# A first stage issued in the order of its text, with the weight splits of the second stage set behind it

## The chip, the cores and the metric

The kernel runs on one core of one Trainium2 chip. The metric is the device time of one execution in microseconds (us). The core has a matrix engine (PE), a vector engine (DVE), an activation engine (ACT), GpSimd (POOL) and a sync engine (SP) whose queue issues the DMAs. Each engine takes its instructions from a queue of its own, in the order in which they stand there.

## The reference, cut to what matters

```python
def _attn_ref(r, k, v, w, u):                 # 4 batches, 8 heads, 768 steps, 48 wide
    for t in range(S):
        cur = einsum('bhd,bhe->bhde', u[None] * kt, vt)
        y[:, :, t] = einsum('bhd,bhde->bhe', rt, state + cur)
        state = wt[:, :, :, None] * state + einsum('bhd,bhe->bhde', kt, vt)

x = attention as 3072 tokens x 384
h = maximum(maximum(x @ w1, x @ w2), x @ w3)   # 384 -> 768
x = h @ w_out                                  # 768 -> 384
h = x @ w_in                                   # 384 -> 2048
out = (h - tanh(h)) @ w_out2                   # 2048 -> 384
```

Weights come as float64 and are turned to float32 on the chip.

## The kernel before, in words

The attention is cut into 24 chunks of 128 steps, six for each batch, and the tokens into six groups of four chunks (512 tokens). Chunks 0 to 3 are computed first. Then group 0 goes through the first two layers while chunks 4 to 7 are computed in between, then group 1 with chunks 8 to 11, and so on. After the six groups a last stage runs the layer of 2048.

A chunk is prepared one chunk ahead, on DVE: two scans over the decays (`scans`, into the single buffers `suf` and `fwd`), two multiplications of keys and receptance (`decays`), and a product for the term with `u` (`bonus`). ACT squares the scans for a range test (`squares`), PE sums the bonus (`bonus_sum`), POOL decays the state (`state_decay`). Then, for the chunk itself, PE makes the scores into banks 4 and 5 (`scores`) and transposes the keys into bank 7 (`key_turn_pe`), ACT copies the keys to `kcn` and the scores to `P` (`masked`), POOL zeroes half of each `P`, DVE puts the bonus on its diagonal from chunk 6 on (`diagonal`), PE adds keys and values to the state (`state_mm`) and computes the outputs (`outputs`), and ACT takes them out (`outputs_out`, for which the first chunks need one copy over 96 partitions and three over 32). From chunk 8 on the keys are turned by a DVE transpose and a trip through DRAM (`key_turn`, `key_order`) and not on PE.

Group 0 uses float32 weights `WAg` and `WOg` as they come. One unit is 128 x 384 weights: `w1_load` fetches it, `w1_unit` converts it, one ACT instruction (L66) and four on DVE (L72 to L75). There are 18 units of `WAg` and 6 of `WOg`. In group 0 a unit of `WAg` feeds three matmuls (L639), a slot; the maximum over three slots goes to `h0`, and 18 matmuls over `WOg` (L666) end the group. Later groups use each weight as two parts, high and low: `wA_split` and `wO_split` (both `split`, L433 and L434) make them from `WAg` and `WOg`, a cast on ACT and a subtraction on POOL (even units) or DVE (odd units). Every matmul of the later groups needs its unit's two parts (L443 to L445).

The text gives an order, but what stands in a queue is decided when the program is built: a scheduler sets each instruction where it reckons the engine to be free, so an instruction can stand before others that precede it in the text. The splits of `WAg` and `WOg`, which the text has after the group's last matmuls, stand much earlier in the queues that way.

`PRELOAD` says how many weight units are fetched ahead of chunk 2's loads and how many before chunk 3's, `PRO` how many are converted after each of chunks 0 to 3, `LEAD` how many slots ahead of PE a unit is converted in group 0:

```python
PRO = [0, 1, 3, 4]
LEAD = 3
PRELOAD = [1, 6]
                w1_upto(slot + 1 + LEAD + max(0, slot - 8))
```

Of the kernel before, what the change touches and what calls it, by code (L numbers as in the profile page):

```python
# [10 lines left out]
F32R = mybir.dt.float32r  # L11
# [8 lines left out]
P = 128  # L20
# [19 lines left out]
EARLY_R = [0, 5]  # L40
W2A = 12
MM_BANKS = [0, 1, 2, 3]
PRO = [0, 1, 3, 4]
LEAD = 3
WARM = [12, 4, 2, 0]
PRELOAD = [1, 6]
SLOTS = 8
AC = 64 + HD
VW = NP * 3 * HD
# [42 lines left out]
def main_path(ctx, tc, wT, rkT, w0, rk0, nat, vpad, uT, ub, wA, wo1, wi2, wo2, outT, count):  # L92
# [85 lines left out]
    def ring(c):  # L178
        return c % 3
# [91 lines left out]
    def key_turn_pe(c):  # L271
        if needs_state(c):
            for p in range(NP):
                pe.transpose(dsb[:, p * C:(p + 1) * C], rk[ring(c)][:, 1, p, :], ident)
            act.copy(kcn.rearrange("t b r -> t (b r)"), dsb)


# [97 lines left out]
    def att_steps(c, col):  # L375
        n = c + 1 if c + 1 < NCH else None
        st = {}

        def k0():
            scores(c, st)  # L380
            masked(c, st)
            if n and n < EARLY_B:
                bonus(n)
            if n:
                scans(n)

        def k1():
            if c < KEYS_PE:
                key_turn_pe(c)
            if c >= EARLY_B:  # L390
                diagonal(c)
            if n:
                decays(n)
                if n >= EARLY_B:
                    bonus(n)
                squares(n)

        def k2():
# [12 lines left out]
        def k4():  # L411
            outputs(c)
            outputs_out(c, col)
            if n and n < EARLY_B:
                bonus_vals(n)
            load_next(c)

        return [k0, k1, k2, k3, k4]

    def in_range():  # L420

# [33 lines left out]
    def warm(n):  # L455

        for _ in range(n):
            pe.matmul(bank[3], zeros[:, 0:P], zeros, start=True, stop=True)

    zeros = xs[:, KT - 1, 256:512].bitcast(BF16)  # L460
    pool.memset(zeros, 0.0)
    warm(WARM[0])
# [16 lines left out]
    def w1_load(i):  # L479
        sp.dma_start(Yi[:, (i % SLOTS) * 2 * UN:(i % SLOTS + 1) * 2 * UN], w1raw[i].bitcast(I32))  # L480
# [43 lines left out]
    for c in range(GROUPS[0]):  # L524
        st = {}
        n = c + 1
        scores(c, st)
        key_turn_pe(c)
        masked(c, st)
        warm(WARM[2] if c < 2 else 0)  # L530
        state_mm(c)
        bonus(n)
        scans(n)
        decays(n)
        state_add(c)
        state_decay(n)
        outputs(c)
        warm(WARM[3] if c < 2 else 0)
        outputs_out(c, c * C)
        squares(n)  # L540
        load_next(c)
        if c == 0:
            sp.dma_start(ubt, ub)
            for i in range(PRELOAD[1], SLOTS):
                w1_load(i)
        for _ in range(PRO[min(c, len(PRO) - 1)]):
            w1_unit()
        bonus_sum(n)
        bonus_vals(n)
# [38 lines left out]
    def y_split(g, d):  # L588
# [2 lines left out]
        act.copy(hi[:, d], src)  # L591
        dve.tensor_tensor(lo[:, d], src, hi[:, d], ALU.subtract)

    c0 = 0
    for g, gn in enumerate(GROUPS):
        n = gn * C
        lastg = g == len(GROUPS) - 1
        nchunks = [] if lastg else list(range(c0 + gn, c0 + gn + GROUPS[g + 1]))
        steps = [s for i, c in enumerate(nchunks) for s in att_steps(c, i * C)]
        nslots = 3 * F1  # L600
        if g == len(GROUPS) - 2:
            def w2_open():
# [18 lines left out]
        def advance(slot):  # L621
            nonlocal done
            want = min(len(steps), -(-len(steps) * (slot + 1) // nslots))
            while done < want:
                if steps[done]:
                    steps[done]()
                done += 1
            if g == 0:
                w1_upto(slot + 1 + LEAD + max(0, slot - 8))
            if g == 1:  # L630
                wA_split(slot + 1 + SPLIT_LEAD)

        slot = 0
        for f in range(F1):
            for j in range(3):
                bk = mm()
                for k in range(KT):
                    if g == 0:
                        pe.matmul(bk, WAg[3 * f + j][:, k], x0[:, k], start=k == 0, stop=k == KT - 1)  # L639
                    else:  # L640
                        mm3(bk[:, 0:n], WAh[:, f, j, k], WAl[3 * f + j][:, k], xh[:, k, 0:n], xl[:, k, 0:n],
                            k == 0, k == KT - 1)
                if j == 0:
                    t = tmp()
                    act.copy(t[:, 0:n], bk[:, 0:n])
                else:
                    dve.tensor_tensor(h0[:, f] if g == 0 and j == 2 else t[:, 0:n], bk[:, 0:n], t[:, 0:n], ALU.max)  # L647
                if j == 2 and g:
                    act.copy(hh[:, f, 0:n], t[:, 0:n])  # L649
                    (dve if f == F1 - 1 else pool).tensor_tensor(hl[:, f, 0:n], t[:, 0:n], hh[:, f, 0:n], ALU.subtract)  # L650
                advance(slot)
                slot += 1
        if lastg:
# [7 lines left out]
            w2_queue(units)  # L661
        for d in range(KT):
            bk = mm()
            for f in range(F1):
                if g == 0:
                    pe.matmul(bk, WOg[:, d, f], h0[:, f], start=f == 0, stop=f == F1 - 1)  # L666
                    continue
                mm3(bk[:, 0:n], WOh[:, d, f], WOl[:, d, f], hh[:, f, 0:n], hl[:, f, 0:n], f == 0, f == F1 - 1)
            if lastg:
                y_split(0, d)  # L670
                w2_step()
            elif d == 0:
                if g == 0:
                    xh = shared.tile([P, KT, 512], F32R, name="xh", tag="xh")
                x_split(GROUPS[g + 1] * C)
            act.copy(ys(d, g), bk[:, 0:n])  # L676
            if g == 0:
                wO_split(2 * d)
                wO_split(2 * d + 1)
                wA_split(SPLIT_B * (d + 1))  # L680
        if g == 0:
            hh, hl = (shared.tile([P, F1, 512], F32R, name=t, tag=t) for t in ("hh", "hl"))
# [242 lines left out]
```

## Time and profile before

| what | us |
|---|---|
| median of 3 runs | 881.69 (881.02 to 881.86) |
| the profiled execution | 885.45 |
| its span, first to last instruction | 883.7 |
| PE busy | 847.8 |
| DVE busy | 503.3 |
| ACT busy | 328.6 |
| POOL busy | 196.4 |

Busy time is the union of an engine's instructions. Matmuls are pipelined and their ends are modelled, so that a stretch in which PE waits a little inside a row of matmuls still reads as busy. The granted clock of PE is given as a share of its full 2.4 GHz; its other level is 1.2 GHz.

### The profile page before, as it was taken

How to read it: one execution, taken by the hardware profiler on the slowest of the kernel's cores; microseconds unless marked ns; L12 is line 12 of the kernel's file. 1: busy time of each engine (PE TensorE's matmuls, PEld its weight loads, DVE VectorE, ACT ScalarE, POOL GpSimd, SP SyncE). 2: the span in 40 equal slices, each digit the busy share in tenths (PEclk: the TensorE clock that was granted, in tenths of full speed). 3: DMA queues.
4: the chain of work that ended last, by engine and by line, in shares of the span. 5: the costliest groups of instructions: out<-in, count | busy, mean ns of one | idle time of the engine just before them, and what ended most of it. 6: DMA issues, size and time to landing. Idle time of an engine off the chain costs nothing.

```text
span 883.7 us, 11938 instructions
## 1 busy us (share of the span) xinstructions
PE 847.8 (96%) x4482; PEld 650.9 (74%) x4482; DVE 503.3 (57%) x824; ACT 328.6 (37%) x647; POOL 196.4 (22%) x201
## 2 busy tenths in 40 slices
PE   7889689999999999999998999999999999999996
PEld 5755344777777777778876688888888888888884
DVE  8879893674574764747999734334334334333332
ACT  4554432334334243335455423234223224323222
POOL 6443560352442442420253300000000000000000
PEclk8799889999999999999999999999999999999999
DMA  9555323234235244215534100000000000000001
GB/s 266 149 208 161 106 80 96 75 104 145 69 115 140 76 129 134 83 25 155 145 98 137 36 0 36 1 1 36 1 1 36 0 1 36 1 0 36 1 1 39
DMA packets 39120, 65.42 MB, mean 74 GB/s; under 512 B 6096, under 2 KB 20176, under 8 KB 39056
## 3 DMA queue, kind: packets, MB, share of 16 engines
q1 hardware_dynamic: 39056, 64.59, 24.4%
q8 instruction: 37, 0.61, 0.3%
q14 instruction: 27, 0.22, 0.1%
HBM read 52.71 MB, written 8.13 MB: 69 GB/s over the span
## 4 chain that ended last, share of the span: by engine, by line
PE 81%; DVE 9%; issue 3%; POOL 3%; DMA 2%; ACT 1%; SPq 0%; ACTq 0%; DVEq 0%; POOLq 0%
PE bank L443 24%; PE bank L445 23%; PE bank L444 23%; PE bank L352 3%; PE bank L639 2%; PE bank L283 2%; PE bank L666 2%; PE bank L316 1%; DVE cv L75 1%; DVE suf L207 1%; DVE fwd L209 1%; DVE WAg L75 1%; POOL WO2l L434 1%; DVE cv L74 1%; POOL WOl L434 0%
## 5 line engine op out<-in xcount | busy, mean ns | idle before, releaser
L703 DVE TENSOR_TENSOR tmp<-bank,tmp 128x512 f32<-128x512 f32 x96 | 66.3, 690 | 174.5 <-ACT tmp L702 174.5
L702 ACT ACTIVATE tmp<-bank 128x512 f32<-128x512 f32 x96 | 57.5, 599 | 182.6 <-PE bank L445 182.6
L443 PE MATMUL bank<-hh,WO2h 128*128 128x512 f32 x288 | 114.2, 397 | 1.7 <-ACT hh L704 1.6
L445 PE MATMUL bank<-hl,WO2h 128*128 128x512 f32 x288 | 114.2, 397 | 0.7 <-DVE hl L705 0.5
L444 PE MATMUL bank<-hh,WO2l 128*128 128x512 f32 x288 | 113.6, 394 | 0.0
L443 PE MATMUL bank<-xh,WAh 128*128 128x512 f32 x270 | 111.1, 412 | 0.0
L445 PE MATMUL bank<-xl,WAh 128*128 128x512 f32 x270 | 106.8, 395 | 0.0
L444 PE MATMUL bank<-xh,WAl 128*128 128x512 f32 x270 | 106.4, 394 | 0.0
L705 DVE TENSOR_TENSOR hl<-tmp,hh 128x512 fp32r<-128x512 f32 x96 | 66.4, 692 | 59.1 <-PE bank L445 46.7
L704 ACT CAST hh<-tmp 128x512 fp32r<-128x512 f32 x96 | 59.5, 620 | 72.7 <-DVE tmp L703 72.6
L445 PEld LDWEIGHTS bank<-hl,WO2h 128*128 128x128 f32 x288 | 54.1, 188 | 16.0 <-DVE hl L705 3.3
L443 PEld LDWEIGHTS bank<-hh,WO2h 128*128 128x128 f32 x288 | 54.2, 188 | 15.6 <-ACT hh L704 3.2
L444 PEld LDWEIGHTS bank<-hh,WO2l 128*128 128x128 f32 x288 | 54.2, 188 | 12.9
L650 POOL TENSOR_TENSOR hl<-tmp,hh 128x512 fp32r<-128x512 f32 x25 | 39.6, 1584 | 101.5 <-ACT hh L649 101.5
L443 PEld LDWEIGHTS bank<-xh,WAh 128*128 128x128 f32 x270 | 50.8, 188 | 15.0 <-issue 2.1
L288 DVE COPY_PREDICATED P<-dmask,sd 128x512 f32<-128x512 uint8 x36 | 32.3, 945 | 49.1 <-POOL P L300 49.1
L445 PEld LDWEIGHTS bank<-xl,WAh 128*128 128x128 f32 x270 | 50.8, 188 | 11.9
L444 PEld LDWEIGHTS bank<-xh,WAl 128*128 128x128 f32 x270 | 50.9, 188 | 10.4 <-issue 0.2
L639 PE MATMUL bank<-x,WAg 128*128 128x512 f32 x108 | 55.1, 658 | 0.0
L647 DVE TENSOR_TENSOR tmp<-bank,tmp 128x512 f32<-128x512 f32 x66 | 44.9, 681 | 12.2 <-PE bank L445 11.7
L649 ACT CAST hh<-tmp 128x512 fp32r<-128x512 f32 x30 | 18.5, 617 | 76.7 <-DVE tmp L647 76.7
L443 PE MATMUL bank<-xh,W2ha 128*128 128x512 f32 x108 | 43.0, 398 | 2.9 <-ACT Yb L676 2.9
(201 smaller groups left out, 1616.0 us busy)
## 6 DMA issues: line engine op xcount, KB each, us to landing
Y<-in_wA SPq DMA_DIRECT2D x18, 384.0 KB, 6.4
nt<-in_nat SPq DMA_DIRECT2D x12, 576.0 KB, 4.6
rk<-in_rkT SPq DMA_DIRECT2D x30, 192.0 KB, 3.4
w2st<-in_wi SPq DMA_DIRECT2D x12, 384.0 KB, 3.3
third<-in_nat SPq DMA_DIRECT2D x7, 576.0 KB, 4.7
kbd<-fwd SPq DMA_DIRECT2D x13, 256.0 KB, 2.1
fwd<-kbd SPq DMA_DIRECT2D x52, 64.0 KB, 2.0
third<-in_rkT SPq DMA_DIRECT2D x16, 192.0 KB, 3.3
```

Source lines behind the costliest of these rows:

```text
L288: dve.copy_predicated(q, dmask[:, None, :].to_broadcast([P, NP, C]), sdt[c % 2][:, j::2, None].to_broadcast([P, NP, C]))
L352: pe.matmul(yab[64 * j:64 * j + HD, p * C:(p + 1) * C], *t(j), start=i == 0, stop=i == len(terms) - 1)
L443: pe.matmul(bk, wh, ah, start=first, stop=False)
L444: pe.matmul(bk, wl, ah, start=False, stop=False)
L445: pe.matmul(bk, wh, al, start=False, stop=last)
L639: pe.matmul(bk, WAg[3 * f + j][:, k], x0[:, k], start=k == 0, stop=k == KT - 1)
L647: dve.tensor_tensor(h0[:, f] if g == 0 and j == 2 else t[:, 0:n], bk[:, 0:n], t[:, 0:n], ALU.max)
L650: (dve if f == F1 - 1 else pool).tensor_tensor(hl[:, f, 0:n], t[:, 0:n], hh[:, f, 0:n], ALU.subtract)
L702: act.activation(t, bk, AF.Tanh)
L703: dve.tensor_tensor(t, bk, t, ALU.subtract)
L704: act.copy(hh[:, r], t)
L705: dve.tensor_tensor(hl[:, r], t, hh[:, r], ALU.subtract)
```

## The change

`tc.manual_schedule()` is opened before the first instruction and closed after the last matmuls of group 0. What is written between stands in every queue in the order of the text; the scheduler may still set later work, of group 1, between it. For that order the text is written anew: `PRO` and `PRELOAD` have other numbers, the key copy is a step of its own (`key_out_pe`), the steps of chunks 4 to 7 are cut into six (`i0` to `i5`), the maxima of group 0 are taken one slot late (`max0`), conversions keep four units ahead of PE, the last conversions of `WOg` stand between the matmuls of L741, and the splits come with one `d` delay.

```diff
-PRO = [0, 1, 3, 4]
+PRO = [0, 0, 1, 2]
-PRELOAD = [1, 6]
+PRELOAD = [0, 4]
...
+        def i0():
+            scores(c, st)
+            if n < EARLY_B:
+                bonus(n)
+            scans(n)
+        def i1():
+            key_turn_pe(c)
+            masked(c, st)
+            decays(n)
...
+        def i2():
+            key_out_pe(c)
+            if c >= EARLY_B:
+                diagonal(c)
+            squares(n)
+        def i3():
+            state_mm(c)
+            bonus_sum(n)
+        def i4():
+            outputs(c)
+            state_add(c)
...
+            state_decay(n)
...
+        def i5():
+            outputs_out(c, col)
+            load_next(c)
...
+    in_order = ExitStack()
+    in_order.enter_context(tc.manual_schedule())
...
+    def max0(f, j, bk):
+        if j == 0:
+            act.copy(h0[:, f], bk)
+        else:
+            dve.tensor_tensor(h0[:, f], bk, h0[:, f], ALU.max)
...
-                w1_upto(slot + 1 + LEAD + max(0, slot - 8))
+                w1_upto(slot + 1 + LEAD)
...
+                if g == 0:
+                    late.append((f, j, bk))
+                    advance(slot)
+                    if len(late) > 1:
+                        max0(*late.pop(0))
+                    slot += 1
+                    continue
...
+            if g == 0:
+                w1_upto(3 * F1 + 2 * d + 4)
+                if d:
+                    act.copy(ys(d - 1, g), bks[-1])
+                    wO_split(2 * d - 2)
+                    wO_split(2 * d - 1)
+                    wA_split(SPLIT_B * d)
...
+            in_order.close()
```

Three places in the queues show it. The first is ACT around chunk 6's key copy, in the second half of group 0. `WAh` and `WOh` are the high parts, `Y` holds the raw weights, `P` the scores. Before:

```order
L433 CAST WAh_101<-WAg16_118 128x384
L66 ACTIVATE WOg_126<-Y_100 128x384
L363 COPY yst1_152<-bank6_91 112x512
L433 CAST WAh_101<-WAg17_119 128x384
L66 ACTIVATE WOg_126<-Y_100 128x384
L433 CAST WOh_120<-WOg_126 128x384
L66 ACTIVATE WOg_126<-Y_100 128x384
L645 COPY tmp1_133<-bank1_86 128x512
L433 CAST WOh_120<-WOg_126 128x384
L299 COPY P0_145<-bank4_89 128x512
L299 COPY P1_146<-bank5_90 128x512
L275 COPY kcn_147<-bank7_92 128x512
```

Now, at the same key copy:

```order
L366 COPY yst1_152<-bank6_91 112x512
L66 ACTIVATE WAg11_113<-Y_100 128x384
L478 CAST WAh_101<-WAg11_113 128x384
L302 COPY P0_145<-bank4_89 128x512
L302 COPY P1_146<-bank5_90 128x512
L66 ACTIVATE WAg12_114<-Y_100 128x384
L278 COPY kcn_147<-bank7_92 128x512
```

The key copy stood behind the casts of the last units of `WAg` and the first of `WOg`, which wait for DVE's conversions of these; now the last conversion ahead of it is that of unit 11. The casts of units 4 to 17 are still set early among the work of group 0, those of `WOg` and of units 0 to 3 are not.

The second place is PE at the end of group 0. Before, its last unit, chunk 7's outputs (left out), the 18 matmuls over `WOg` and the first of group 1:

```order
L639 MATMUL bank1_86<-x0_123,WAg17_119 128x512 x3
...
L666 MATMUL bank2_87<-h0_125,WOg_126 128x512 x6
L666 MATMUL bank3_88<-h0_125,WOg_126 128x512 x6
L666 MATMUL bank0_85<-h0_125,WOg_126 128x512 x6
L443 MATMUL bank1_86<-xh_991,WAh_101 128x512
```

Now (L286 are chunk 8's scores, L319 its state, L355 its outputs):

```order
L703 MATMUL bank1_86<-x0_123,WAg17_119 128x512 x3
L741 MATMUL bank2_87<-h0_125,WOg_126 128x512 x3
L286 MATMUL bank4_89<-third_141 128x128
L286 MATMUL bank5_90<-third_141 128x128
...
L319 MATMUL bank7_92<-third_141,kcn_147 48x48 x8
L355 MATMUL bank6_91<-third_141,AS0_148 48x128 x2
L355 MATMUL bank6_91<-P0_145,third_141 48x128
L355 MATMUL bank6_91<-P1_146,third_141 48x128
...
L741 MATMUL bank2_87<-h0_125,WOg_126 128x512 x2
```

Chunk 8's matmuls, which stood in group 1, now part the first three of these 18 from the others; the last six stand among the first of group 1.

The third place is DVE at the same time. Before, behind the masks of chunk 7 (L288), with all of `WOg` converted:

```order
L288 COPY_PREDICATED P0_145<-dmask_94,sd1_154 128x512
L288 COPY_PREDICATED P1_146<-dmask_94,sd1_154 128x512
L647 TENSOR_TENSOR h0_125<-bank2_87,tmp0_132 128x512
L434 TENSOR_TENSOR WAl15_1381<-WAg15_117,WAh_101 128x384
L259 STREAM_TRANSPOSE fwd_143<-third_141 128x512
```

Now, from chunk 8's key transpose on, with five of the six units of `WOg` still to convert:

```order
L259 STREAM_TRANSPOSE fwd_143<-third_141 128x512
L207 SCALAR_TENSOR_TENSOR suf_142<-wt0_135,d1_144 128x517
...
L291 COPY_PREDICATED P0_145<-dmask_94,sd0_153 128x512
L209 SCALAR_TENSOR_TENSOR fwd_143<-wt0_135,d1_144 128x516
L72 TENSOR_SCALAR WOg_126<-WOg_126 128x384
L291 COPY_PREDICATED P1_146<-dmask_94,sd0_153 128x512
L73 TENSOR_SCALAR WOg_126<-WOg_126 128x384
L216 TENSOR_TENSOR rk0_137<-rk0_137,fwd_143 128x512
L74 SCALAR_TENSOR_TENSOR WOg_126<-Y_100,WOg_126 128x384
```

The second unit of `WOg` is converted between the scans of chunk 9 and the masks of chunk 8. From the later part of group 1 on, every queue stands as before.

## Rows read from the trace of the kernel before

**Rows 1.** The page's first part: busy us, share of the span, instructions.

```profile
PE 847.8 (96%) x4482; PEld 650.9 (74%) x4482; DVE 503.3 (57%) x824; ACT 328.6 (37%) x647; POOL 196.4 (22%) x201
```

**Rows 2.** Busy us (and instructions) by stage, with granted clock, DMA share, GB/s.

```profile
core 0: us, PE busy (x) PEld busy (x) DVE busy (x) ACT busy (x) POOL busy (x), PEclk, DMA share, GB/s
...
9.40:53.70 44.30, 34.56 (x297) 30.73 (x297) 38.50 (x65) 25.03 (x67) 19.01 (x23) 0.81 0.74 221
53.70:136.80 83.10, 71.69 (x367) 38.07 (x365) 72.88 (x129) 32.25 (x74) 40.91 (x36) 0.90 0.37 117
136.80:152.60 15.80, 15.80 (x40) 7.14 (x39) 3.54 (x7) 4.91 (x11) 2.00 (x2) 1.00 0.39 122
152.60:220.00 67.40, 67.40 (x464) 53.10 (x463) 41.88 (x61) 23.96 (x50) 26.57 (x27) 1.00 0.36 104
```

**Rows 3.** PE's waits in 53 to 137: us in total, times, longest.

```profile
PE bank L316 <- ACT kcn L275: 11.4, 2, 7.8
```

**Rows 4.** Timeline of ACT: start, us, instruction, idle before.

```profile
97.50 0.51 ACT L433 CAST WAh<-WAg 128x384 fp32r<-128x384 f32 x1 [4.23 <-DVE WAg L75]
...
103.57 0.60 ACT L275 COPY kcn<-bank 128x512 f32<-128x512 f32 x1
```

**Rows 5.** Timeline of PE from the first unit of group 0 on.

```profile
53.67 4.50 PE L639 MATMUL bank<-x,WAg 128*128 128x512 f32 x6
...
76.03 10.57 PE L639 MATMUL bank<-x,WAg 128*128 128x512 f32 x24
...
105.03 6.99 PE L639 MATMUL bank<-x,WAg 128*128 128x512 f32 x12
...
136.79 15.72 PE L666 MATMUL bank<-h,WOg 128*128 128x512 f32 x36
```

**Rows 6.** Timeline of PE: the last output matmuls of chunks 0 to 3.

```profile
20.17 0.38 PE L341 MATMUL bank<-P,nt 128*96 128x128 f32 x2
...
33.49 0.38 PE L341 MATMUL bank<-tmp,nt 128*96 128x128 f32 x2
...
40.92 0.38 PE L341 MATMUL bank<-P,third 128*96 128x128 f32 x2
...
49.49 0.38 PE L341 MATMUL bank<-tmp,nt 128*96 128x128 f32 x2
```

**Rows 7.** Timeline of ACT in chunk 2's and 3's turn.

```profile
42.73 0.79 ACT L360 COPY x<-bank 32x128 f32<-32x128 f32 x3
...
44.47 1.07 ACT L299 COPY tmp<-bank 128x512 f32<-128x512 f32 x2
```

**Rows 8.** Groups by line in 53.7 to 136.8: busy us, mean ns, idle before.

```profile
L639 PE MATMUL bank<-x,WAg 128*128 128x512 f32 x108 | 55.1, 658 | 0.0
...
L75 DVE SCALAR_TENSOR_TENSOR WAg<-Y,WAg 128x384 int32<-128x384 int32 x10 | 7.2, 724 | 0.0
...
L300 POOL TENSOR_SCALAR_AFFINE_SELECT P<-P 128x512 f32<-128x512 f32 x8 | 7.0, 893 | 10.3 <-ACT P L299 10.3
L74 DVE SCALAR_TENSOR_TENSOR WAg<-Y,WAg 128x384 int32<-128x384 int32 x10 | 6.2, 625 | 0.0
L434 DVE TENSOR_TENSOR WAl<-WAg,WAh 128x384 fp32r<-128x384 f32 x9 | 5.4, 605 | 0.1
L72 DVE TENSOR_SCALAR WAg<-WAg 128x384 f32<-128x384 f32 x10 | 5.3, 541 | 1.1 <-ACT WAg L66 1.1
...
L288 DVE COPY_PREDICATED P<-dmask,sd 128x512 f32<-128x512 uint8 x4 | 5.1, 1323 | 2.0 <-POOL P L300 2.0
...
L73 DVE TENSOR_SCALAR WAg<-WAg 128x384 int32<-128x384 int32 x10 | 4.4, 452 | 0.1
...
L207 DVE TENSOR_TENSOR_SCAN suf<-wt,d 128x517 f32<-128x517 f32 x3 | 3.7, 1228 | 0.8 <-POOL AS L245 0.8
...
L434 DVE TENSOR_TENSOR WOl<-WOg,WOh 128x384 fp32r<-128x384 f32 x3 | 2.3, 759 | 0.0
```

**Rows 9.** Timeline: chunk 8's keys, from their transpose to their copy.

```profile
128.34 0.70 DVE L259 STREAM_TRANSPOSE fwd<-third 128x512 f32<-128x512 f32 x1
...
134.55 0.62 ACT L268 COPY kcn<-fwd 128x512 f32<-128x512 f32 x1 [7.87 <-DMA fwd<-kbd]
```

More of the change, by code (lines that the diff above doesn't have):

```diff
@@ L274, in key_turn_pe, with key_out_pe @@
                 pe.transpose(dsb[:, p * C:(p + 1) * C], rk[ring(c)][:, 1, p, :], ident)
+    def key_out_pe(c):
+        if needs_state(c):
             act.copy(kcn.rearrange("t b r -> t (b r)"), dsb)
@@ L416, in k4 @@
             load_next(c)
-        return [k0, k1, k2, k3, k4]
+        if c >= 2 * GROUPS[0]:
+            return [k0, k1, k2, k3, k4]
+        def i0():
[7 more added lines that the diff above has]
+            decays(n)
+            if n >= EARLY_B:
+                bonus(n)
+        def i2():
+            key_out_pe(c)
+            if c >= EARLY_B:
[7 more added lines that the diff above has]
+            state_add(c)
+            if n >= KEYS_PE:
+                key_turn(n)
+                key_order(n)
+            state_decay(n)
+            if n < EARLY_B:
+                bonus_vals(n)
+        def i5():
+            outputs_out(c, col)
+            load_next(c)
+        return [i0, i1, i2, i3, i4, i5]
     def in_range():
@@ L528, in main_path @@
         key_turn_pe(c)
+        key_out_pe(c)
         masked(c, st)
@@ L542, in main_path @@
         if c == 0:
-            sp.dma_start(ubt, ub)
             for i in range(PRELOAD[1], SLOTS):
                 w1_load(i)
+        if c == 2:
+            sp.dma_start(ubt, ub)
         for _ in range(PRO[min(c, len(PRO) - 1)]):
@@ L599, in main_path @@
         steps = [s for i, c in enumerate(nchunks) for s in att_steps(c, i * C)]
+        if g == 0:
+            steps = []
+            for i, c in enumerate(nchunks):
+                a = att_steps(c, i * C)
+                if steps:
+                    steps[-1] = (lambda x, y: lambda: (x(), y()))(steps[-1], a.pop(0))
+                steps += a
         nslots = 3 * F1
@@ L628, in advance @@
             if g == 0:
-                w1_upto(slot + 1 + LEAD + max(0, slot - 8))
+                w1_upto(slot + 1 + LEAD)
             if g == 1:
                 wA_split(slot + 1 + SPLIT_LEAD)
-        slot = 0
+        slot, late = 0, []
         for f in range(F1):
@@ L646, in main_path @@
                 else:
-                    dve.tensor_tensor(h0[:, f] if g == 0 and j == 2 else t[:, 0:n], bk[:, 0:n], t[:, 0:n], ALU.max)
-                if j == 2 and g:
+                    dve.tensor_tensor(t[:, 0:n], bk[:, 0:n], t[:, 0:n], ALU.max)
+                if j == 2:
                     act.copy(hh[:, f, 0:n], t[:, 0:n])
@@ L652, in main_path @@
                 slot += 1
+        while late:
+            max0(*late.pop(0))
         if lastg:
@@ L661, in main_path @@
             w2_queue(units)
+        bks = []
         for d in range(KT):
@@ L671, in main_path @@
                 w2_step()
-            elif d == 0:
-                if g == 0:
-                    xh = shared.tile([P, KT, 512], F32R, name="xh", tag="xh")
+            elif d == 0 and g:
                 x_split(GROUPS[g + 1] * C)
+            elif d == 1 and not g:
+                xh = shared.tile([P, KT, 512], F32R, name="xh", tag="xh")
+                x_split(GROUPS[g + 1] * C)
+            if g == 0:
+                w1_upto(3 * F1 + 2 * d + 4)
[4 more added lines that the diff above has]
+                    wA_split(SPLIT_B * d)
+                bks.append(bk)
+                continue
             act.copy(ys(d, g), bk[:, 0:n])
[L677 to L680, printed above, removed]
         if g == 0:
+            act.copy(ys(KT - 1, g), bks[-1])
+            wO_split(2 * KT - 2)
+            wO_split(2 * KT - 1)
+            in_order.close()
             hh, hl = (shared.tile([P, F1, 512], F32R, name=t, tag=t) for t in ("hh", "hl"))
```

## The prediction

> **What bounds the kernel now.** I read the page's first part, then the windows by stage, then PE's waits, then the timelines of PE and ACT where PE stands idle. PE is busy 847.8 of 883.7 us [rows 1], so that 35.9 us are open, and the windows show where: PE is idle 9.7 us between 9.4 and 53.7 (chunks 0 to 3, stage A here) and 11.4 us between 53.7 and 136.8 (the 18 units of group 0, stage B), and not at all from there to 220 [rows 2]. Clock is lost too: the granted clock is 0.81 in A and 0.90 in B, a mix of the two levels, and 1.00 afterwards [rows 2]. From 136.8 on PE goes through its work without a gap, and the rows of the queues are the same again from the later part of group 1 on. So the change is worth the PE time that it saves or loses up to there, and the rest of the program moves with it.
>
> In B the whole 11.4 us is one wait, `state_mm` of chunks 6 and 7 for the key copy, 7.8 us at worst [rows 3]. ACT made that copy at 103.57; ahead of it stood casts for the splits, and the one at 97.50 had itself stood 4.23 us for DVE's conversion of its unit [rows 4]. ACT's queue shows how: in the order of before that copy is behind the casts of units 16 and 17 and of `WOg`. Nothing of group 0 needs those casts.
>
> **Stage A.** It ends when unit 0 starts, at 53.7, and that unit takes 4.50 us [rows 5], where four take 10.57 at full clock (2.64 each), so it loses another 1.9. The last outputs of chunks 0 to 3 end at 20.4, 33.7, 41.2 and 49.7 (the last starts, with two steps of about 0.2 [rows 6]): turns of 13.3, 7.4 and 8.6. The first of these fell where the clock was low. In text order a turn is one chain: ACT takes the outputs out (three of the four copies 0.79 [rows 7], about 1.3 in all), squares twice, copies the bonus sum; only then may PE transpose into bank 7, ACT copy keys and scores (1.07 for two [rows 7]), POOL mask them (0.9 each [rows 8]) and PE form the outputs. I estimate 8.8 at full clock, between the turns seen. Chunk 0 gains: its score copies now follow its transposes and not a square of chunk 1, so I put its end at 17.5. With turns of 10.5, 10 and 9.6 (one still partly at low clock; the last holds a conversion) and 1.4 for the last copies, unit 0 starts at 49.0. **A gives 4.7.** Bounds: 45 with all turns at 8.8 to 9 and chunk 0 ending at 17; 57 with two turns of 13.3 and no gain in chunk 0. The order of loads (chunk 2 ahead of the weight units) is costed at nothing: three units are converted before the slots now, against eight before, and four fetched ahead cover that; if chunk 2's loads were late, its turn would be.
>
> **Stage B.** PE's own work here: busy 71.7 [rows 2], of which 55.1 are the unit matmuls [rows 8], which at 2.64 each need 47.6. So 64.2 at full clock. DVE's work: 72.9 busy before [rows 2]. Out go its splits (nine of `WAl` 5.4, three of `WOl` 2.3 [rows 8]) and the preparation of one chunk that now falls behind the stage (two scans of 1.23 [rows 8] and two multiplications, about 3.8). In come two more conversions, since 18 of the 24 stand here against 16; one costs 2.3 (7.2, 6.2, 5.3 and 4.4 for ten of each of its four instructions [rows 8]), together 4.6. So 66.0. PE and DVE come out as good as equal, and with conversions kept four units ahead neither can run off. I take 68.5, DVE's work and 2.5 for its waits on ACT and POOL. **B gives 83.1 - 68.5 = 14.6.** Bounds: 64.2, PE alone, if DVE's instructions get shorter as POOL's splits leave the stage; 76.2, if DVE keeps the 10.2 us of idle time that it has now (83.1 - 72.9). The maxima into `h0` are as many as before, one slot later: nothing, since the slot behind them covers them; without it each would add its 0.7 to PE's wait.
>
> **Stage C, the end of group 0.** Before, the 18 matmuls run in one piece, 15.7 us [rows 5]. Now chunk 8's scores, state and outputs stand behind the third of them. That work is only moved, but its waits are new. From the end of the scores to the last mask: a copy 0.5, a mask on POOL 0.9, a predicated copy 1.3, a scan 1.2, a small conversion step 0.5, the second predicated copy 1.3 (all [rows 7, 8]), 5.7 together, under which PE has `state_mm` alone (about 0.5). PE stands some 5.0, and all matmuls of `WOg` behind it. The keys of chunk 8 need their trip through DRAM, 6.2 from transpose to copy [rows 9]; PE has two units, chunk 7's outputs, three matmuls and the scores to cover it, over 10, so I cost it at nothing; if DVE is late by more than about 3, the excess comes out on PE. Then the fifth and sixth units of `WOg` are converted between chunk 9's masks and chunk 10's scan: 4.6 and 3.9 and small pieces, some 10, against about 6 of matmuls in front, with DVE partly ahead: 2.5. Last the clock: after the 7.8 us of idle time, two units took 6.99 and not 5.28 [rows 3, 5]; I take 2.0 for the stalls here. **C costs 9.5**, bounds 3 (DVE and POOL ahead, clock kept) and 14 (keys late too). The splits themselves, now at the head of group 1, I cost at nothing: DVE is busy 41.9 and POOL 26.6 of 67.4 there [rows 2], a unit of group 1 needs nine matmuls, and two splits per two units take 0.6 on DVE and about 1.2 on POOL. If that cover fails, PE waits at its first units of group 1.
>
> **The sum.** -4.7 - 14.6 + 9.5 = -9.8. The profiled execution took 885.45, 3.8 above the median of the runs; on its own scale that is 875.7, on that of the runs 881.69 - 9.8 = **871.9**.
>
> **The rivals.**
> *DVE follows PE freely, and C is covered.* B is 64.2 and C costs 4: -4.7 - 18.9 + 4 = -19.6, 862.1. For it: POOL is busy 40.9 in B and loses its splits [rows 2], and DVE's instructions there are slow for their size (0.72 for L75 against 0.62 for L74 of the same shape [rows 8]). Against: the waits in C stand in the queues. The Trainium skill, SBUF — State Buffer, "SBUF: two separate sides", states that VectorE and GpSimd lock one port pair against each other for a whole instruction. By that rule fewer splits on POOL shorten DVE's work, which leads to this case and its 862.1; the spread between L75 and L74 agrees with it but no row here takes the two engines apart.
> *Stage A stays at the low clock.* Unit 0 starts at 57, by the turn of 13.3 twice: +3.3 - 14.6 + 9.5 = -1.8, 879.9. For it: 13.3 was seen and the clock of 0.81 in A [rows 2, 6]; against: two turns of before were at 7.4 and 8.6 with gaps as well. The Trainium skill, TensorE: Matmul & The Clock Gate, "HAM oscillation", says that matmul bursts with waits between them start cold each time. That speaks against this change, as its turns are bursts; the trace agrees for the first turns and the 6.99, not for the later ones.
> *Slower: conversions wait in place.* DVE meets each conversion in its turn, behind masks that wait for POOL, for ACT, for scores; no other unit can be taken meanwhile, PE waits at its slot, and the next maximum waits for PE. With A and C as above the change is no gain from a B of 78.3 on, which is 4.35 us for each of 18 slots (83.1 / 18 = 4.6 before, 3.8 in my sum). At 4.8 a slot B is 86.4: -4.7 + 3.3 + 9.5 = +8.1, 889.8. For it: ACT's 4.23 us behind a conversion [rows 4], and casts of units 4 to 17 still stand in its queue; against: DVE stood idle only 10.2 in all in B before [rows 2]. The PSUM page of the Trainium skill (PSUM — Partial Sum Buffer, "Engine vs sequencer instructions") calls these queues strict first in, first out; the row at 97.50 agrees.
> *No change.* C eats all: the keys come late, the splits start late, 19 instead of 9.5. About 881.5. Against: it needs each cover of C to fail at once.
>
> **Chances.** A change under 0.2% (1.8 us) can't be told from none here. Forecast, 866 to 877: 0.50. DVE free: 0.20. Low clock in A: 0.13, a fourth of which falls within 0.2%. No change: 0.06. Slower: 0.11. That makes faster 0.80, same 0.09, slower 0.11. From 860 to 881 lie the forecast, three quarters of the second case and most of the third, about 0.8; the forecast's own range is 866 to 877.
>
> **What would show it.** A: unit 0 between 45 and 57 (49). B: unit 0 to the first matmul over `WOg` 64 to 76 (68.5), no wait of `state_mm` for the key copy above 1 us, DVE busy 90% and more. C: PE waiting for DVE's predicated copy (L291) by 3 us or more between the third and fourth of the 18, a lower clock behind it. After that, the rest at before's pace. I am wrong in B if PE's waits there sum to over 10 us, and in the splits if PE waits for `WAl` in group 1.

## The result and the profile after

The changed kernel is slower: 893.15 us (890.88 to 893.58, median of 4) against 881.78 (881.02 to 883.58) in the same session, a ratio of 1.0121 [1.0098, 1.0144]. The forecast was 871.9, the range 860 to 881. The profiled execution took 893.23, its span is 891.3.

The stages after (columns as in [rows 2]; the third and fourth rows together are stage C, from the first of the 18 matmuls over `WOg` to ACT's last of three copies of group 1's outputs):

```profile
core 0: us, PE busy (x) PEld busy (x) DVE busy (x) ACT busy (x) POOL busy (x), PEclk, DMA share, GB/s
9.40:56.00 46.60, 38.04 (x301) 33.38 (x301) 24.93 (x37) 16.64 (x45) 16.80 (x22) 0.74 0.58 168
56.00:133.30 77.30, 70.77 (x368) 37.31 (x369) 70.66 (x120) 33.51 (x80) 23.46 (x25) 0.93 0.50 143
133.30:165.90 32.60, 27.07 (x128) 14.56 (x126) 27.32 (x47) 14.51 (x32) 12.38 (x13) 0.84 0.41 116
165.90:226.97 61.07, 60.29 (x369) 46.75 (x368) 40.70 (x59) 20.65 (x44) 27.70 (x27) 1.00 0.31 88
```

A ends at 56.0 (2.3 later than before), B takes 77.3 (5.8 less), C takes 93.7. The same stretch of before is 136.8 to 218.36, 81.6 long and all of it PE busy at full clock, so C costs 12.1: 6.3 of idle PE (93.7 - 87.4) and 5.8 of PE busy for longer, at a lower clock. Together -5.8 + 2.3 + 12.1 = +8.6. What follows takes 664.3, against 665.3 before. PE's longest waits in C:

```profile
PE bank L741 <- DVE WOg L75: 2.5, 1, 2.5
PE bank L319 <- ACT kcn L268: 1.7, 1, 1.7
PE bank L355 <- ACT yst L366: 0.9, 1, 0.9
```

The spans of the two profiled executions differ by 7.6 us, the medians by 11.4: the profiled execution of before was 3.8 above its median, that of the changed kernel lay at its own. Kernel e1 below (the changed text, all ordered by the scheduler) is as fast as before, and its profiled execution lies at its median (882.33 to 882.08); against its stages (51.4, 82.8, 81.4, rest 664.7) the change costs 4.6 in A, gains 5.5 in B, costs 12.2 in C and gains 0.3 in the rest, together 11.0.

A is the stage to look at first. DVE is busy 24.9 of 46.6 us where it was 38.5 of 44.3 [rows 2]. Its waits in 9.4 to 56, and PE's (us in total, times, longest):

```profile
DVE suf L207 <- ACT yst L249: 11.5, 2, 6.3
DVE WAg L72 <- ACT WAg L66: 4.8, 1, 4.8
DVE rk L215 <- POOL nt L221: 2.3, 1, 2.3
```

```profile
PE bank L274 <- ACT sd L233: 4.0, 3, 1.6
```

DVE has nothing to do while its next scan waits for ACT's squares. Before, eight units were converted in A and 16 in B. Now one stands in A, 18 in B, where DVE is busy 91%, and five in C. Its conversions in B (busy, mean ns, idle before) and PE's waits there:

```profile
L75 DVE SCALAR_TENSOR_TENSOR WAg<-Y,WAg 128x384 int32<-128x384 int32 x17 | 12.7, 745 | 0.6
L74 DVE SCALAR_TENSOR_TENSOR WAg<-Y,WAg 128x384 int32<-128x384 int32 x17 | 12.3, 726 | 0.6
L72 DVE TENSOR_SCALAR WAg<-WAg 128x384 f32<-128x384 f32 x17 | 8.1, 475 | 5.8 <-ACT WAg L66 5.8
L73 DVE TENSOR_SCALAR WAg<-WAg 128x384 int32<-128x384 int32 x17 | 7.4, 433 | 0.6
```

```profile
PE bank L703 <- DVE WAg L75: 3.5, 2, 1.9
PE bank L703 <- DVE h L648: 3.0, 1, 3.0
```

The key copy's 11.4 us [rows 3] are gone, and DVE has taken their place: 17 units of `WAg` cost 40.5 us, 2.38 each.

### The profile page after: what moved, and what is told of

Same layout as the page of the kernel before. It is cut to its first block, busy times and chain, and to the rows that moved or that the text cites. A ratio compares the mean times of both kernels' runs of the same rounds, so it can differ in the third digit from the quotient of the medians.

```text
span 891.3 us, 11912 instructions
## 1 busy us (share of the span) xinstructions
PE 854.3 (96%) x4482; PEld 653.1 (73%) x4482; DVE 509.4 (57%) x824; ACT 328.3 (37%) x647; POOL 191.5 (21%) x201
## 3 DMA queue, kind: packets, MB, share of 16 engines
q1 hardware_dynamic: 39056, 64.59, 24.9%
## 4 chain that ended last, share of the span: by engine, by line
PE 70%; DVE 8%; POOL 2%; DMA 2%; issue 2%; SPq 1%; ACT 1%; DVEq 0%; POOLq 0%; ACTq 0%
PE bank L488 22%; PE bank L490 21%; PE bank L489 21%; PE bank L355 2%; PE bank L286 1%; PE bank L703 1%; POOL WAl L479 1%; DVE cv L75 1%; DVE tmp L719 1%; DVE fwd L209 1%; DVE suf L207 1%; POOL WO2l L479 1%; PE bank L319 1%; DVE WAl L479 1%; DVE cv L74 1%
## 5 line engine op out<-in xcount | busy, mean ns | idle before, releaser
L788 DVE TENSOR_TENSOR tmp<-bank,tmp 128x512 f32<-128x512 f32 x96 | 66.3, 691 | 174.5 <-ACT tmp L787 174.5
L790 DVE TENSOR_TENSOR hl<-tmp,hh 128x512 fp32r<-128x512 f32 x96 | 66.4, 692 | 59.1 <-PE bank L490 46.6
L488 PEld LDWEIGHTS bank<-hh,WO2h 128*128 128x128 f32 x288 | 54.2, 188 | 15.7 <-ACT hh L789 3.5
L489 PEld LDWEIGHTS bank<-hh,WO2l 128*128 128x128 f32 x288 | 54.2, 188 | 12.9
L703 PE MATMUL bank<-x,WAg 128*128 128x512 f32 x108 | 54.2, 647 | 6.6 <-DVE WAg L75 3.5
L291 DVE COPY_PREDICATED P<-dmask,sd 128x512 f32<-128x512 uint8 x36 | 30.5, 890 | 37.8 <-POOL P L303 37.8
L719 DVE TENSOR_TENSOR tmp<-bank,tmp 128x512 f32<-128x512 f32 x60 | 40.8, 680 | 11.5 <-PE bank L490 11.0
```

What stands on the lines that cost most here:

```text
L291: dve.copy_predicated(q, dmask[:, None, :].to_broadcast([P, NP, C]), sdt[c % 2][:, j::2, None].to_broadcast([P, NP, C]))
L488: pe.matmul(bk, wh, ah, start=first, stop=False)
L489: pe.matmul(bk, wl, ah, start=False, stop=False)
L719: dve.tensor_tensor(t[:, 0:n], bk[:, 0:n], t[:, 0:n], ALU.max)
L788: dve.tensor_tensor(t, bk, t, ALU.subtract)
L790: dve.tensor_tensor(hl[:, r], t, hh[:, r], ALU.subtract)
```

## The experiments

All are compared with the kernel before, run beside them. Stages as above, in us; for kernels that end the fixed order elsewhere the bounds are the same instructions.

| kernel | A ends | B | first of the 18 | C | ratio to before |
|---|---|---|---|---|---|
| before | 53.7 | 83.1 | 136.8 | 81.6 | 1 |
| changed | 56.0 | 77.3 | 133.3 | 93.7 | 1.0121 [1.0098, 1.0144] |
| e1 all by the scheduler | 51.4 | 82.8 | 134.2 | 81.4 | 0.9993 [0.9976, 1.0009] |
| e2 only A in text order | 60.6 | 77.6 | 138.2 | 86.5 | 1.0097 [1.0065, 1.0129] |
| e3 only B and C in text order | 48.6 | 70.5 | 119.1 | 95.0 | 1.0000 [0.9981, 1.0018] |
| e4 eight conversions in A | 53.5 | 67.9 | 121.4 | 95.9 | 1.0027 [1.0010, 1.0044] |
| e5 conversions in pairs | 55.5 | 72.9 | 128.4 | 95.3 | 1.0068 [1.0044, 1.0092] |
| e6 = e4 and e5 | 54.2 | 65.4 | 119.6 | 96.0 | 1.0029 [1.0014, 1.0045] |
| e7 more warm matmuls in A | 52.6 | 74.8 | 127.4 | 97.2 | 1.0099 [1.0071, 1.0127] |
| e8 `WOg` within the slots | 53.5 | 85.0 | 138.5 | 90.3 | 1.0170 [1.0140, 1.0201] |
| f1 order ends before the 18 | 53.4 | 86.1 | 139.5 | 89.2 | 1.0182 [1.0153, 1.0211] |
| f2 = e6 and f1 | 54.6 | 73.7 | 128.3 | 88.3 | 1.0032 [1.0014, 1.0050] |
| f3 = f1, A by the scheduler, pairs | 50.4 | 77.3 | 127.7 | 89.7 | 1.0034 [1.0020, 1.0047] |
| f4 bonus sum ahead of outputs | 71.5 | 74.3 | 145.8 | 94.6 | 1.0311 [1.0281, 1.0341] |
| g1 = e6 and e8 | 56.2 | 73.7 | 129.9 | 94.5 | 1.0096 [1.0077, 1.0114] |
| g2 = g1, A by the scheduler | 52.6 | 73.4 | 126.0 | 95.4 | 1.0032 [1.0015, 1.0049] |
| g3 squares later | 53.7 | 74.6 | 128.3 | 95.0 | 1.0117 [1.0092, 1.0141] |
| g4 = g1 and g3 | 54.5 | 73.6 | 128.1 | 94.5 | 1.0087 [1.0067, 1.0108] |
| h1 order ends in group 1 | 55.0 | 75.6 | 130.6 | 105.5 | 1.0239 [1.0214, 1.0264] |
| h2 = h1 and e6 | 53.8 | 65.4 | 119.2 | 108.7 | 1.0146 [1.0120, 1.0172] |

None beats before beyond the intervals. The changed kernel, e5, e8, f1 and h1 have the same text up to the end of A; it ended at 53.4 to 56.0 there, with a granted clock of 0.74 to 0.85 (one trace of each). So differences in A of under 2.6 us tell nothing, the 2.3 by which the changed kernel's A ends later than before among them.

**Which part of the fixed order costs.** e1 drops it, e2 closes it ahead of the first slot, e3 opens it there:

```diff
-    in_order.enter_context(tc.manual_schedule())    # e1, e3
...
     scb.items, scb.i = scb.items[0:2], 0
+    in_order.close()                                # e2
+    in_order.enter_context(tc.manual_schedule())    # e3
```

> The text of the changed kernel, but the order on each engine is again the scheduler's from first to last. Theory 1 (the fixed order is what costs): conversions go back into VectorE's gaps, so the first 227 us come out as before or a little better, the key wait of 7.8 us partly gone by the other edits (the maxima one slot later, the later WOg conversions): 878 to 883. Rival (the other edits of the text cost, above all chunk 8's work between the 18 matmuls and the splits put behind them): it stays near 890 to 893, and the end of group 0 shows the cost of about 12 us.

> Text order for chunks 0 to 3 alone; from the first unit on the scheduler orders. The changed kernel lost 2.3 us in stage A, won 5.8 in B and lost 12.1 in C. If these add up by stage, A stays at 56.0, and B and C stand as they would with the scheduler's order: with three conversions instead of eight before the first unit, VectorE has five more (11.9 us at 2.38) in B, so B is 83 or more and the total 882 + 2.3 + 0 to 5 = 884 to 889. Rival (the loss of C comes from the text, not from the fixed order): C still loses 12 us, total 895 or more.

> The scheduler orders chunks 0 to 3, text order from the first unit to the end of group 0. Theory 1 (conversions that lie in VectorE's gaps in A make B shorter): the text asks for three units before the slots, so the scheduler has nothing more to bring forward than the text's own three and whatever of the first slots it may move up; A is 51 to 54 and the total 888 to 891. Rival (A's loss is the low clock that any order meets with these edits): A stays at 56, total 893.

e1: 882.08, so the other edits of the text neither cost nor gain by themselves. With the order fixed in A the kernel takes 891.04 (e2) and 893.15 (changed), with A by the scheduler 882.08 (e1) and 881.90 (e3): fixing A costs 9 and 11 us, whatever comes after. Both theories on e3 were too high, and the windows show why:

```profile
9.40:48.60 39.20, 32.10 (x292) 29.29 (x292) 28.23 (x46) 18.49 (x50) 15.38 (x21) 0.83 0.66 195
48.60:119.10 70.50, 65.90 (x368) 35.45 (x368) 62.08 (x108) 31.25 (x74) 22.19 (x23) 1.00 0.54 156
119.10:214.12 95.02, 85.83 (x493) 61.00 (x494) 69.74 (x109) 35.24 (x76) 41.21 (x41) 0.96 0.33 97
```

A and B together come to 119.1, near the 117.5 of the forecast; but C takes 95.0, 13.4 more than before, and the medians show no gain at all. e1 refutes that C's cost lies in the text (81.4). In e2, with the order fixed in A alone, C takes 86.5.

**Conversions in A.** e4 puts them where DVE is idle; e5 makes two units at a time, each step for both before the next; e6 has both.

```diff
-PRO = [0, 0, 1, 2]
+PRO = [0, 2, 3, 3]
...
         state_decay(n)
+        for _ in range(PRO[c]):
+            w1_unit()
         outputs(c)
```

> The changed kernel with eight instead of three conversions before the first unit, each set between the state decay and the outputs of its chunk, where VectorE stood idle (21.7 of stage A's 46.6 us). Theory 1 (the conversions moved out of A make VectorE the bound of B): five conversions of 2.38 us leave B, so B falls from 77.3 to about 68 to 71, A stays at 56 to 57; total 885 to 887. Rival (A's chain on ScalarE and its low clock set the time, and each conversion put there lengthens a turn): A grows by 5 or more, B falls by 7, total 891 to 893. Second rival (B is bound by trips between engines, not by VectorE's amount of work): B stays above 75 and the total is 893 or more.

> The changed kernel with the four steps of two conversions alternated on VectorE in the 18 slots (two units each second slot), so that no step follows at once on the one whose result it reads. Theory 1b (dependent steps back to back cost VectorE about 0.36 us a unit: 1.84 against 1.48): some 20 units give 7 us of VectorE's time, of which B keeps 3 to 6; total 887 to 890. Rival (the difference between 1.84 and 1.48 comes from GpSimd's work beside them, or VectorE doesn't bound B): no change, 892 to 894, or worse, as two units at once hold up masks and maxima by 2 us.

> Eight conversions in stage A between state decay and outputs, and pairs alternated, both edits together. Theory 1 with 1b: B goes to PE's own bound, 66 to 69, A 56; total 882 to 885, so that the fixed order no longer loses in A and B and C's 12 us remain. Rival (the gains are the same time counted twice): the total equals that of the better one of the two alone.

e4: 884.83. A isn't longer for the conversions (53.5, within its spread), and B falls by 9.4 to just under the 68 expected. Its B, and DVE's wait for the squares in A (11.5 in the changed kernel):

```profile
53.50:121.40 67.90, 65.83 (x368) 35.45 (x368) 56.83 (x95) 29.84 (x72) 23.87 (x23) 1.00 0.51 143
```

```profile
DVE suf L207 <- ACT yst L249: 3.4, 1, 3.4
```

So conversions put back into DVE's gaps of A regain 8.3 of the 11.4 us that the change lost; the kernel is still slower than before by 1.0 to 4.4 in a thousand. Two other kernels limit what this shows. In e2 the scheduler put eight conversions into A as well, and there A ends at 60.6 and 9 us are lost: it seems to count where in A they stand. And e3 has only three in A, 16 in B, and is as fast as before, with an A that ends at 48.6. e5: 888.11, and DVE's busy time in B falls from 70.66 to 64.31 with one instruction more (120, now 121): 6.35 over the 18 units that are converted there is 0.35 a unit, where 0.36 was expected. Its B:

```profile
55.50:128.40 72.90, 67.69 (x370) 36.32 (x370) 64.31 (x121) 33.70 (x80) 22.19 (x25) 0.98 0.52 155
```

e6 brings B to PE's own bound, but not the total (884.58, as e4). Its B and C:

```profile
54.20:119.60 65.40, 65.40 (x369) 35.72 (x370) 52.73 (x97) 30.13 (x73) 23.15 (x23) 1.00 0.52 149
119.60:215.63 96.03, 86.78 (x494) 61.40 (x493) 62.40 (x103) 35.09 (x76) 42.88 (x42) 0.95 0.33 96
```

**The clock and ACT's queue in A.** e7 sets four warm matmuls into all four turns. f4 and g3 take ACT's copy of the bonus sum out from behind other work: f4 moves `bonus_sum` and `bonus_vals` ahead of the outputs, g3 moves the squares behind them.

```diff
-        warm(WARM[2] if c < 2 else 0)      # e7, with WARM = [12, 4, 4, 0]
+        warm(WARM[2])
...
+        bonus_sum(n)                       # f4
+        bonus_vals(n)
         outputs(c)
...
-        squares(n)                         # g3
         bonus_sum(n)
         bonus_vals(n)
+        squares(n)
```

> The changed kernel with four matmuls over zeros in each of the turns of chunks 0 to 3, behind the masks (before: two in the first two turns). Theory 2 (stage A's loss is the low clock, which PE's idle time brings: the outputs' steps take 0.43 instead of 0.22 us in parts of all four turns): the granted clock of stage A rises from 0.74 to 0.80 or more and A ends 2 to 4 us earlier, total 889 to 891. Rival (the chain of copies on ScalarE sets the turn and PE's own speed hardly counts): A within 1 us of 56, total 892 to 894.

> The changed kernel with the bonus sum of the next chunk and its copy put before the outputs of the chunk in the text of chunks 0 to 3, so that the next transposes no longer wait for a copy that stands behind the outputs' copies and the squares on ScalarE (4.0 us of waits in three turns). Theory 2b (that chain lengthens A): A ends 2.5 to 4 us earlier, at 52 to 53.5, total 889 to 891. Rival (the bonus product, which VectorE makes late, now stands ahead of the outputs and holds them; or the clock decides): A at 55 to 57, total 892 to 894.

> The changed kernel with the two squares of the next chunk set behind the copy of its bonus sum in the text of chunks 0 to 3, so that the copy, for which PE's transposes wait, stands two ScalarE instructions earlier (about 1.6 us with their accumulator reads). Theory 2b (the ScalarE queue ahead of the copy is a term of A): PE's 4.0 us of waits for that copy shrink to under 1.5 and A ends 1.5 to 4 us earlier, total 889 to 892. Rival (VectorE's next scan waits for the squares, 11.5 us in two waits in the changed kernel, and is now later still): A at 56 or more, total 893 to 897.

e7: 890.71 and a clock of 0.88 in A, but an end of 52.6 is barely outside the spread and the interval overlaps that of the changed kernel: inconclusive. g3: 892.05, no difference in the total, though PE's waits for the copy fell from 4.0 to 0.2 us; waits for POOL's masks took their place (6.2, in the changed kernel 2.6). f4: 908.98, a miss:

```profile
PE bank L232 <- DVE S L329: 15.9, 3, 6.9
```

The bonus sum goes into the bank of the state matmuls, so it must wait for DVE's addition of the state (L329), which stands behind the next chunk's scans; with the outputs queued behind it, A is 15 us longer.

**Stage C.** e8 converts all of `WOg` within the slots (the term `max(0, slot - 8)` put back); g1 does so with e6, where DVE has time to spare, and g2 does it with A by the scheduler. f1 ends the fixed order before the 18 matmuls, f2 and f3 are f1 with what gained in B.

```diff
-                w1_upto(slot + 1 + LEAD)
+                w1_upto(slot + 1 + LEAD + max(0, slot - 8))    # e8, g1, g2
...
+        if g == 0:                                             # f1, f2, f3
+            in_order.close()
         bks = []
```

> The changed kernel with all WOg units converted within the slots of group 0, as before the change, so that no conversion stands between chunk 9's masks and chunk 10's scan. Theory 3 (conversions in C hold up the 18 matmuls): three conversions of 2.38 us move from C to B; C's cost falls from 12 by 3 to 7, B grows by 3 to 7, the total within 2 us of 893 but the stages different. Rival (C's cost is the order of chunk 8's masks and predicated copies alone): C's cost stays at 11 to 12 and B grows, total 896 to 900.

> The changed kernel with the fixed order ended before the 18 matmuls over WOg instead of behind them; chunks 0 to 3 and the slots stay in text order. Theory 3 (the fixed order of the 18 matmuls with conversions and splits between them costs the 12 us from their start to the end of group 1, by PE's 6.3 us of waits and 5.8 us of low clock): that stretch comes back from 93.7 to 82 to 87, A and B stay at 56 and 77, total 881 to 887. Rival (the stretch pays for what B hands it late, whatever the order in it, as it grew to 95 and 96 in the kernels whose B was shorter): it stays above 91, total 891 or more.

> Three edits of the changed kernel together: eight conversions in stage A between state decay and outputs, conversions in pairs, the fixed order ended before the 18 matmuls. If the three gains are each the gain of its own stage: A 54, B 65.4, from the 18 matmuls to the end of group 1 82 to 86, rest 664.6, so a span of 866 to 870 and a total of 868 to 872, faster than both kernels by some 10 us. Rival (what B saves comes back as waits in the last stretch, since loads and VectorE's backlog set the pace from chunk 0 to group 1): total 880 to 884.

> Chunks 0 to 3 by the scheduler, the slots of group 0 in text order with conversions in pairs, the rest by the scheduler again. By stages: A 48.6, B 66 to 70, the last stretch 82 to 86, rest 664.6: span 861 to 869, total 863 to 871. Rival as before: what is saved comes back in the last stretch, total 878 to 882.

> Fixed order to the end of group 0 as in the changed kernel, with eight conversions in stage A, conversions in pairs, and all WOg units converted within the slots. There VectorE had 12.7 us to spare in B (52.7 busy of 65.4), and three conversions more need some 6.3. If C's cost is the WOg conversions that stand between its matmuls: A 54, B 66 to 68, from the 18 matmuls to the end of group 1 86 to 91, total 873 to 880, faster than both kernels. Rival (C's cost is chunk 8's own chain of scores, masks and keys, which needs its time whenever B ends): that stretch stays at 95 to 96, total 883 to 887.

> Chunks 0 to 3 by the scheduler with eight conversions as before the change, from the first slot to the end of group 0 the text order, conversions in pairs, all WOg units within the slots. By stages A 51 to 54, B 66 to 68, the last stretch 86 to 91: total 870 to 880. Rival as in the kernel beside it: last stretch 95 to 96, total 880 to 886.

e8: 896.54; C falls by 3.4 and B grows by 7.7. In g1 and g2 no conversion is left in C, and C stays at 94.5 and 95.4 (e6: 96.0), so the conversions between the matmuls are not the main cause. B came to 73.7 and 73.4 there, not to the 66 to 68 expected. (g4 had 889.54 and the same C.) PE's longest wait in C is now that for the keys, in g1 and g2 alike; before it had none there:

```profile
PE bank L333 <- ACT kcn L282: 5.4, 2, 3.8
```

f1: 898.03; C falls by 4.5, and the splits, no longer held behind the fixed order, go back into B. DVE's and POOL's groups in B:

```profile
L479 DVE TENSOR_TENSOR WAl<-WAg,WAh 128x384 fp32r<-128x384 f32 x8 | 5.3, 661 | 0.0
...
L479 POOL TENSOR_TENSOR WAl<-WAg,WAh 128x384 fp32r<-128x384 f32 x8 | 9.9, 1242 | 15.7 <-DVE WAl L479 8.8 <-PE bank L703 6.8
```

B is 86.1 with them. So the order's end also sets what may stand in the slots; f2 and f3 (885.59, 884.86; B 73.7 and 77.3) are no faster than e6 for what seems the same reason.

The last two leave PE its queue of before at this place: the fixed order ends five slots into group 1, the 18 matmuls are one piece, and chunk 8's work stands behind units of group 1.

```diff
                 advance(slot)
                 slot += 1
+                if g == 1 and slot == 5:
+                    in_order.close()
```

> The changed kernel with the fixed order kept five slots longer, into group 1, so that PE's queue there is the same row for row as before the change: the 18 matmuls over WOg in one piece, chunk 8's scores, state and outputs each behind a unit of group 1. Theory 3b (what costs the 12 us is that chunk 8's work, left to the scheduler, stands between the third and fourth of the 18 matmuls, each of its waits bare, and the clock falls there): from the first of the 18 to the end of group 1 it comes back from 93.7 to 82 to 87, A and B stay at 54 to 56 and 77, total 880 to 886. Rival (VectorE and ScalarE are late with WOg, the splits and chunk 8's masks whatever PE's order): it stays above 91, total 890 or more.

> As the kernel beside it, with eight conversions in stage A and conversions in pairs. By stages, if theory 3b holds: A 54, B 65.4, from the 18 matmuls to the end of group 1 82 to 87, rest 664.6, so a span of 866 to 871 and a total of 868 to 874, faster than both kernels. Rival (what B saves comes back behind it): total 880 to 886.

Theory 3b falls: 902.91 and 894.60, C at 105.5 and 108.7 with PE's queue as before. Three timelines of h2 show a chain (its line numbers differ: L282 is the copy of chunk 8's keys, L667 the maximum):

```profile
124.97 0.62 ACT L282 COPY kcn<-fwd 128x512 f32<-128x512 f32 x1 [11.14 <-DMA fwd<-kbd]
125.49 0.58 ACT L665 COPY h<-bank 128x512 f32<-128x512 f32 x1
125.97 0.59 ACT L380 COPY yst<-bank 112x512 f32<-112x512 f32 x1
126.45 1.00 ACT L66 ACTIVATE WOg<-Y 128x384 f32<-128x384 f32 x2
```

```profile
127.04 0.80 DVE L71 TENSOR_SCALAR WOg<-WOg 128x384 f32<-128x384 f32 x2 [7.98 <-ACT WOg L66]
```

```profile
131.82 14.38 PE L762 MATMUL bank<-h,WOg 128*128 128x512 f32 x26 [8.18 <-DVE h L667]
```

ACT's queue stands 11.14 us at a copy whose keys PE takes only behind the 18 matmuls, and behind it are the start of a maximum and of two conversions, on which DVE and then PE wait. In the changed kernel ACT stands at another copy, with a conversion behind it:

```profile
137.20 1.07 ACT L302 COPY P<-bank 128x512 f32<-128x512 f32 x2 [10.29 <-PE bank L286]
138.16 0.63 ACT L268 COPY kcn<-fwd 128x512 f32<-128x512 f32 x1
138.68 0.57 ACT L66 ACTIVATE WOg<-Y 128x384 f32<-128x384 f32 x1
139.15 0.58 ACT L646 COPY h<-bank 128x512 f32<-128x512 f32 x1
```

```profile
158.89 4.37 PE L741 MATMUL bank<-h,WOg 128*128 128x512 f32 x6 [2.54 <-DVE WOg L75]
```

But there the chain isn't shown to reach PE. DVE's one long gap is in front of chunk 8's predicated copy, for POOL's mask, and from it to the conversion that PE waits for at 158.89 DVE works without a gap:

```profile
138.59 1.14 DVE L291 COPY_PREDICATED P<-dmask,sd 128x512 f32<-128x512 uint8 x1 [3.82 <-POOL P L303]
```

Before, ACT stood 7.87 us for the key copy as well [rows 9], but with all of `WOg` converted and the maxima's copies ahead of it.

## Why the prediction was wrong, step by step

The forecast was -9.8, the spans gave +7.6: A was 7.0 longer than forecast, B 8.8, C 2.6, and the rest 1.0 shorter. The steps that failed are the sizes of A and of B.

- **Stage A, 49.0: measured 56.0.** Chunk 0's outputs end at 20.5 as before, not at 17.5, and the later turns took 10.5, 11.0 and 12.9 where the forecast had 10.5, 10 and 9.6. The low-clock rival (57) came nearest; the granted clock was 0.74. PE's rows show it in chunk 3's outputs, with the low clock in the first two rows:

```profile
52.71 0.63 PE L342 MATMUL bank<-ident,nt 128*96 128x128 f32 x2
53.14 0.63 PE L343 MATMUL bank<-tmp,nt 128*96 128x128 f32 x2
...
54.56 0.38 PE L343 MATMUL bank<-tmp,nt 128*96 128x128 f32 x2
54.78 0.38 PE L344 MATMUL bank<-tmp,nt 128*96 128x128 f32 x2
```

Steps start 0.43 apart there and 0.22 at full clock. Fifteen such steps in the last two turns make some 3.2 of the 4.3 us by which these are over, eight in chunk 0 some 1.7 of its 3.0; this is an estimate from the rows. That the clock is the cause is not shown: e7 had 0.88 and an A of 52.6, too near to the spread. That each link of ACT's chain costs its length was wrong too: g3 took 3.8 us of one wait away and others filled in.
- **The conversions: priced at 4.6 in B, as a pure count.** The count of 18 in B was right, though of the three that the forecast had ahead of the slots two began only after unit 0. What the forecast doesn't see is that A gets no shorter without the conversions: with eight in DVE's waits for ACT it ends at 53.5 (e4), with one at 53.4 to 56.0, while in B each is on the bound. Putting them back regains 8.3 us; among the experiments only A by the scheduler (e3) regains more.
- **Stage B, 68.5: measured 77.3, past the bound of 76.2.** DVE's busy time came to 70.7 and not 66.0. The 16 conversions in B had cost 34.7 us before (23.1 for ten of `WAg` [rows 8], 11.6 for six of `WOg`), 2.17 each; 18 cost 43.5 now (40.5, and 3.0 for one of `WOg`), so +8.8 stood where the forecast had +4.6. e5 shows a cause: the kernel's text has the four steps of one unit in a row, and that costs 0.35 a unit; the queue of before alternated the steps of two units for all of `WOg` and part of `WAg`. DVE's idle time was 6.6 and not 2.5 (5.8 of it for ACT's L66), and PE's clock 0.93. Right were the end of the key copy's wait, DVE busy over 90%, and PE waiting less than 10 us.
- **Stage C, 9.5: measured 12.1, within its bounds.** The term that was mis-sized is the clock, 5.8 against 2.0. The waits came to 6.3 (7.5 in the forecast). PE waited 2.5 for `WOg`, as forecast. Chunk 8's work made 3.0 instead of 5.0: the wait for the predicated copy, given as 3 us or more, was 0.4, that for the keys, costed at nothing, 1.7, and that for ACT 0.9.
- **The sum.** e3 and e6 reach the A and B of the forecast (119.1 and 119.6 against 117.5) and end with a ratio of 1.000 and 1.003. So even with the first two steps right, the forecast was 10 us off. One part is C: with the order fixed to the end of group 0 and B at 65 to 75 it takes 94 to 97 (e3 to e7, f4, g1 to g4), 3 to 6 more than the forecast's price, and less only with a longer B (93.7 at 77.3; 90.3 at 85.0, in e8). Another is the scale: the forecast worked its 9.8 out from an execution that was 3.8 above the median and took it off the median.
- **The rival that had the sign,** conversions that wait in their place, gave 889.8 by a B of 86.4. Its tipping point, 4.35 us a slot, was nearly reached (77.3 / 18 = 4.29); the rest came from A and C.
- **The rival of a free DVE** didn't come. Although POOL is busy 23.5 us in B where it was 40.9, L75 takes 0.75 (0.72 before) and L74 0.73 (0.62); the predicated copies did get shorter, 0.72 for 1.32.
- **Splits and later pace: right.** No unit of group 1 waited for `WAl`, and the rest takes 664.3 (665.3 before).

**What stays open.** C's 12 to 16 us are not settled by an experiment. The chain through ACT's queue is read from the trace of h2, and no kernel here took the key copy or the score copies out from ahead of `WOg`. A second cause is compatible with the same rows: chunk 8's keys are transposed at 131.64, 1.7 us ahead of the first of the 18 (h2: 118.35, 0.85 ahead), before at 128.34, 8.5 ahead, so that their trip of 6.2 us [rows 9] is no longer over when the state is due. PE's waits for the keys in g1 and g2 speak for it, but no kernel moved the transpose. Nor was it tried why A's clock varies between kernels with the same text, or why A is so much longer in e2 than in e4.

## What to carry to other kernels

When an order is fixed by hand, first list what the scheduler had put into the gaps that the new text leaves empty; that work isn't gone, and here it came to stand where its engine was busy. In a fixed order an early copy that waits for a transfer is to be judged by everything queued behind it on its engine, as h2's trace shows. And gains of neighbouring stages are not to be added up before one kernel shows them together: in e3's trace A and B gained 17.7 us, C lost 13.4 of them, and the median was that of before.

## What was unexpected of the hardware

DVE steps in a row, each of which reads the one before, start later after one another than their durations say. The changed kernel (one unit), and before (the steps of two units in turn):

```profile
107.20 0.34 DVE L72 TENSOR_SCALAR WAg<-WAg 128x384 f32<-128x384 f32 x1
107.58 0.36 DVE L73 TENSOR_SCALAR WAg<-WAg 128x384 int32<-128x384 int32 x1
107.97 0.56 DVE L74 SCALAR_TENSOR_TENSOR WAg<-Y,WAg 128x384 int32<-128x384 int32 x1
108.56 0.56 DVE L75 SCALAR_TENSOR_TENSOR WAg<-Y,WAg 128x384 int32<-128x384 int32 x1
```

```profile
100.34 0.34 DVE L73 TENSOR_SCALAR WOg<-WOg 128x384 int32<-128x384 int32 x1
100.61 0.35 DVE L72 TENSOR_SCALAR WOg<-WOg 128x384 f32<-128x384 f32 x1
100.88 0.54 DVE L74 SCALAR_TENSOR_TENSOR WOg<-Y,WOg 128x384 int32<-128x384 int32 x1
101.35 0.34 DVE L73 TENSOR_SCALAR WOg<-WOg 128x384 int32<-128x384 int32 x1
```

A step of 0.34 is followed after 0.38 where the next one reads it, and after 0.27 where it doesn't; one of 0.54 to 0.56 after 0.59 and 0.47. That is some 0.12 for each dependent step. The Trainium skill, VectorE: DVE Perf Modes, "The DRAIN you can't avoid", says that the next operation does not start until the pipeline has emptied, and that one which is not held starts earlier. The second group of rows agrees, with starts 0.07 us before the end of the step ahead. What holds the dependent steps in the first group, these rows don't show.
